# Four neighbouring tokens per partition, and a delta in three pieces, in a fused cross-covariance attention and channel-mix kernel

## The chip, the cores and the metric

One core of a Trainium2 chip runs the kernel. The metric is the device time of one execution in microseconds; three executions of the kernel before took 506.9, 507.0 and 507.39 us, and their median, 507.0 us, is the time before. The core's engines are named as the profile names them: PE (TensorE; PEld its weight loads), DVE (VectorE), ACT (ScalarE), POOL (GpSimd) and SP (SyncE). POOL and SP issue the DMAs.

## The reference

```
qn = q / (norm(q, axis=1) + 1e-6)             # q, k, v: 4 x 6208 x 256, norms over the tokens
kn = k / (norm(k, axis=1) + 1e-6)
a  = softmax(kn^T @ qn / tau)                 # 256 x 256 for each of the 4 batches
x  = v @ a                                    # 4 x 6208 x 256
x_prev = x moved by one token (zero in front of each batch)
xk = mu_k * x + (1 - mu_k) * x_prev
xr = mu_r * x + (1 - mu_r) * x_prev
out = sigmoid(xr @ w_r) * (relu(xk @ w_k)^2 @ w_v)     # w_k 256 x 1024, w_v 1024 x 256, w_r 256 x 256
```

Inputs and result are float32; the kernel computes the matmuls in bf16.

## The kernel before

**Tiling.** Each batch has 12 blocks of 512 tokens and 64 tokens left over. The blocks of all batches are taken in one list: 48 blocks, and one "left" block of 4 x 64 tokens, put ahead of the last. Channels lie on the partitions (two halves of 128), tokens along the columns.

**What happens to a block.** `v_load` (line 400, the DMA on line 403) brings 512 tokens of v into a buffer `v_bf` as bf16, on POOL's DMA queue. Today partition p holds the tokens p, 128+p, 256+p and 384+p of the block (`"(s p) c -> p s c"`), so a partition reads four rows of 1 KB that lie apart. v is then turned, so that channels are on the partitions: the first five blocks by PE (line 421, copied out of PSUM on lines 427 to 433, the blocks 2 to 4 on line 429 by DVE), all others by a transposing DMA on SP's queue (line 409). `x_stage` multiplies by the softmax matrix A (line 536, ACT copies the product to `xR`, line 542; block 0 has lines of its own, 513 to 526). `xR` is a ring of three blocks side by side, with one column in front, which holds the last token of the block before the ring's first (line 502 copies it there, or line 499 sets it to zero at the start of a batch).

`mix_stage` (line 546) makes xk and xr. Today the columns of `xR` are in the order of the tokens, so "the token before" is the column before. It takes delta = x - x_prev in one DVE instruction over both channel halves (line 576), then for k and for r multiplies delta by mu, one instruction per half (line 590), and adds x_prev (line 599). For block 0 both steps are one instruction (line 584), in two cuts of 256 columns; for the left block lines 574 and 597 do it. `mu` holds four columns, made on PE and copied out of PSUM (line 828).

`up_stage` computes xk @ w_k in four pairs of 128 hidden channels (line 628), ACT takes the relu (line 632), DVE the square (line 634). `down_stage` works on four tiles of 128 tokens: the gate's matmuls (line 682), the eight matmuls with w_v (line 689), tanh on ACT (line 693), and the product on DVE (line 695) into `res`, with tokens on the partitions. A block's `res` is stored by one DMA on SP's queue (line 709), in the same order of tokens as v was read; the last block's goes out in three parts (lines 711 and 716).

**Beside the blocks** the q and k rows of the next batch are loaded (`qk_load`, line 750, POOL's queue; each partition already reads 4 KB in one piece) and their products and norms are taken (`cov_group`: ACT squares on line 765, DVE sums on 768 to 778, PE on line 788), so that the next A is ready when its batch begins. For the first batch this is the head of the kernel (lines 323 to 387), with matmuls that only keep PE at work (line 837).

**What sets the order.** Nothing above runs in the order of the source. Every step is added to a `Plan` with an engine, a cost, a key (its due time, in units of T = 9.6 us a block), and what it reads and writes. `Plan.order` then plays the engines forward, always taking the step with the lowest key among those that are ready, and the instructions are issued in that order. A DMA in the plan takes time for its bytes on its queue; for a DMA that begins after 35.5 us of planned time the plan adds 8 us before it counts as landed, if it waits for a mark of PE's progress (a "gate") or if it is on SP's queue. POOL's loads of v and of q and k have such a gate where the mark is already known when they are added; the earliest have none. `dve(n, mode)` and `act(n)` are the plan's costs.

Of the kernel before, what the change touches and what calls it, by code (L numbers as in the profile page):

```python
# [21 lines left out]
class Plan:  # L22
# [40 lines left out]
    def order(self):  # L63
# [16 lines left out]
        while True:  # L80
# [49 lines left out]
            if s.size:  # L130
                at, took = max(bus[e], end + self.MOVE), s.size / self.RATE
                if t < 5.0:
                    at = max(at, bus["SP"])
                if e == "SP" and bus["POOL"] > at:
                    bus["POOL"] += took
                    took *= 4 if s.name == "turn v" else 2
                bus[e] = at + took
                end = bus[e] + self.LAND
                lanes[e].append(end)
                if t > self.SPARE_FROM and (s.gate or e == "SP"):  # L140
                    end += self.SPARE
# [33 lines left out]
def kernel(  # L175
# [222 lines left out]


    def v_load(n, key, gate=()):  # L400
        b, t = blocks[n]
        i = n % NV
        add("POOL", 0.75, key, lambda: nc.gpsimd.dma_start(  # L403
            v_bf[i], v[b, t * M:(t + 1) * M, :].rearrange("(s p) c -> p s c", p=P)),
            writes=[("v_bf", i)], size=M * C * 4, name="ld v", after=root0, gate=gate)
# [140 lines left out]
    def mix_stage(n, key):  # L546
# [3 lines left out]
        ki, ri = n % 2, n % 3  # L550
        o = {"k": xk[ki], "r": xr[ri]}
        cuts = [(0, 256), (256, 512)] if n == 0 else [(0, m)]
        for c0, c1 in cuts:
# [4 lines left out]
            if left:  # L558
                prev = [xl[:, dh, :, :L] for dh in range(2)]
                xdep = [("xl", b) for b in range(B)]  # L560
            else:
                prev = None
                xdep = [("x", i, 0), ("x", i, 1)]
                xdep += [("x", i - 1, 0), ("x", i - 1, 1)] if i else [("x0",)]
                if n == 1 or c0:
                    xdep += [("x1", 0, 0), ("x1", 0, 1)]
                at = i * M
# [9 lines left out]
            kd = key + c0 * .001  # L577
            unit(kd, lambda dgo=dgo, kd=kd, twice=twice, xdep=xdep: add("DVE", twice, kd, dgo, reads=xdep, writes=[("dl", di)], name="delta"))
            for which in "kr":
                km = kd + (.02 * T if which == "k" else .3 * T)  # L580
                if n == 0:
                    for dh in range(2):
                        col = dh if which == "k" else 2 + dh
                        unit(km, lambda xdep=xdep, which=which, col=col, dh=dh, c0=c0, c1=c1, km=km, w=w: add("DVE", dve(w), km, lambda: nc.vector.scalar_tensor_tensor(
                            o[which][:, dh, c0:c1], dl[di][:, dh, c0:c1], mu[:, col:col + 1], xR[:, dh, at + c0:at + c1], op0=OP.mult, op1=OP.add),
                            reads=xdep + [("dl", di), ("mu",)], writes=[("xk", ki, c0, dh) if which == "k" else ("xr", ri, dh)], name="mix"))
                    continue
                for dh in range(2):
                    col = dh if which == "k" else 2 + dh
                    unit(km, lambda col=col, dh=dh, c0=c0, c1=c1, km=km, w=w: add("DVE", dve(w, 2.77), km, lambda: nc.vector.tensor_scalar_mul(  # L590
                        dm[di][:, dh, c0:c1], dl[di][:, dh, c0:c1], mu[:, col:col + 1]), reads=[("dl", di), ("mu",)],
                        writes=[("dm", di, dh)], name="mix"))

                def mgo(which=which, c0=c0, c1=c1):
                    if left:
                        for dh in range(2):
                            nc.vector.tensor_tensor(v3(o[which][:, dh, :m]), v3(dm[di][:, dh, :m]), prev[dh], op=OP.add)
                    else:
                        nc.vector.tensor_tensor(o[which][:, :, c0:c1], dm[di][:, :, c0:c1], xR[:, :, at + c0:at + c1], op=OP.add)  # L599
                res_ = ("xk", ki, c0) if which == "k" else ("xr", ri)  # L600
                unit(km + .01, lambda mgo=mgo, km=km, twice=twice, res_=res_, xdep=xdep: add("DVE", twice, km, mgo,
                     reads=xdep + [("dm", di, 0), ("dm", di, 1)], writes=[res_] + ([("xk", 0, x, y) for x in (0, 256) for y in range(2)] if n == 2 and which == "k" else [("xr", 0, y) for y in range(2)] if n == 3 and which == "r" else []), name="mix"))

# [63 lines left out]
    def down_tile(n, s, kd, last):  # L667
# [3 lines left out]
        def go():  # L671
# [25 lines left out]
            if last:  # L697
# [7 lines left out]
                else:  # L705
                    b, t = blocks[n]
                    o = out[b, t * M:(t + 1) * M, :].rearrange("(s p) c -> p s c", p=P)
                    if n < NBLK - 1:
# [3 lines left out]
            elif n == NBLK - 1 and s:  # L712
                b, t = blocks[n]
                o = out[b, t * M:(t + 1) * M, :].rearrange("(s p) c -> p s c", p=P)
                s0 = 0 if s == 1 else 2
# [111 lines left out]
    add("PE", (0.1, 0.3), KC - 1, go, reads=[("mu_rows", 0), ("mu_rows", 1), ("ident_f",)], writes=[("vr", 1)], name="mu")  # L827
    add("DVE", TINY, KC - 1, lambda: nc.vector.tensor_copy(mu, vr[1][:, 0:4]), reads=[("vr", 1)], writes=[("mu",)], name="mu")
    softmax(0, KC)
# [116 lines left out]
```

## Time and profile before

The profiled execution took 507.02 us from end to end, and 505.1 us from the first to the last instruction (its span).

| what | profile before |
|---|---|
| time of the profiled execution, and its span | 507.02 us, 505.1 us |
| median of three runs | 507.0 us |
| granted PE clock | 1.00 |
| matmuls line 689 (down), 628 (up), 682 (gate), 536 (x), 788 (cov) | 1536, 742, 384, 188, 294 recorded |
| delta, line 576, 128x1024 bf16 | 47 times, 686 ns |
| mix, line 590 (128x512) and line 599 (128x1024) | 188 times 347 ns; 94 times 688 ns |
| DMA packets | 113,958, 77.36 MB |
| load of v (line 403), issue to landing | 48 times, median 6.3 us |
| store of a block (line 709), issue to landing | 47 times, median 5.3 us |
| load of v, time of the issue on POOL | 754 ns; a load of q or k rows 533 ns |

The busy time of an engine is the union of its instructions' times. Instructions follow each other on DVE faster than they last: an instruction's record runs on for some 0.08 us after the next one has begun, so the distance from start to start is also given where it matters. A few matmul records are missing, which shows where an engine's weight loads are all there and a matmul between them is not.

### The profile page before, as it was taken

What the parts mean: (1) busy time and instruction counts of PE and PEld (TensorE: products, weight loads), DVE (VectorE), ACT (ScalarE), POOL (GpSimd) and SP (SyncE); (2) the same over time, 40 slices, a digit from 0 to 9 for tenths busy, and PEclk for the clock granted to TensorE, in tenths of its full rate; (3) what the DMA queues carried; (4) which work ended last, traced back from release to release, by engine and by line L of the source; (5) the groups of instructions that cost most, each with busy time, mean ns of one, the idle gap of its engine ahead of it and who ended that gap; (6) DMA issues with size and microseconds to landing.
All of it is one profiled execution on the core that took longest, in us unless ns stands there. A gap on an engine that the chain in (4) does not pass through costs nothing.

```text
span 505.1 us, 9492 instructions
## 1 busy us (share of the span) xinstructions
PE 486.7 (96%) x3477; PEld 336.2 (67%) x3536; DVE 424.1 (84%) x979; ACT 407.4 (81%) x582; POOL 102.7 (20%) x174
## 2 busy tenths in 40 slices
PE   2999999999999999999999999999999999999997
PEld 0376676777676766776676676676666666666675
DVE  4569799899889989998879999899779787878974
ACT  6867799898889888888789888888767777777774
POOL 6562322222231211222121122211110111000000
PEclk9999999999999999999999999999999999999999
DMA  9999999999999999999897999996664776542123
GB/s 208 208 206 202 168 165 197 185 192 168 173 183 170 197 146 202 185 151 180 145 169 129 167 191 165 173 172 105 140 112 84 133 126 122 108 96 72 48 80 104
DMA packets 113958, 77.36 MB, mean 153 GB/s; under 512 B 49588, under 2 KB 101496, under 8 KB 113912
## 3 DMA queue, kind: packets, MB, share of 16 engines
q0 software_dynamic: 41776, 38.84, 57.0%
q1 hardware_dynamic: 72136, 37.92, 37.0%
q8 instruction: 27, 0.44, 0.4%
q14 instruction: 19, 0.16, 0.1%
HBM read 78.71 MB, written 25.43 MB: 206 GB/s over the span
## 4 chain that ended last, share of the span: by engine, by line
PE 84%; DMA 6%; DVE 6%; issue 2%; ACT 1%; POOL 0%; DVEq 0%; ACTq 0%; POOLq 0%
PE vr L689 31%; PE kT L628 30%; PE xp L536 8%; PE vr L682 8%; PE s_ps L788 6%; DMA qk<-in_q_dram 3%; DMA qk<-in_k_dram 2%; DMA v_bf<-in_v_dram 2%; DVE kk L634 1%; DVE dm L590 1%; DVE dl L576 1%; ACT kr L632 1%; DVE res L695 1%; DVE xk L599 1%; PE kT L837 0%
## 5 line engine op out<-in xcount | busy, mean ns | idle before, releaser
L632 ACT ACTIVATE kr<-kT 128x1024 bf16<-128x1024 f32 (+1 forms) x200 | 199.7, 1001 | 49.9 <-PE kT L628 46.9
L628 PE MATMUL kT<-xk,w_k 128*128 128x512 bf16 (+1 forms) x742 | 201.2, 372 | 2.7
L689 PE MATMUL vr<-w_v,kk 128*128 128x256 bf16 x1536 | 202.0, 273 | 0.1
L634 DVE TENSOR_TENSOR kk<-kr 128x1024 bf16<-128x1024 bf16 (+1 forms) x200 | 133.9, 671 | 45.2 <-ACT kr L632 45.0
L689 PEld LDWEIGHTS <-kk 128*128 128x128 bf16 x1552 | 151.6, 98 | 20.1 <-DVE kk L634 0.6
L628 PEld LDWEIGHTS <-w_k 128*128 128x128 bf16 x800 | 77.6, 98 | 51.9 <-issue 1.4
L693 ACT ACTIVATE res<-vr 128x256 f32<-128x256 f32 x192 | 74.2, 387 | 14.2 <-PE vr L689 10.3
L695 DVE SCALAR_TENSOR_TENSOR res<-res,vr 128x256 f32<-128x256 f32 x192 | 79.1, 413 | 2.5 <-ACT res L693 2.3
L682 PE MATMUL vr<-w_r,xr 128*128 128x256 bf16 x384 | 73.3, 273 | 0.1
L765 ACT ACTIVATE sq<-qk 128x2048 bf16<-128x2048 bf16 (+1 forms) x39 | 70.6, 1810 | 1.2 <-PE xp L798 0.6
L542 ACT CAST xR<-xp 128x512 bf16<-128x512 f32 x94 | 55.3, 589 | 15.2 <-PE xp L536 14.4
L403 POOL DMA_DIRECT2D v_bf<-in_v_dram x48 | 36.2, 754 | 146.8 <-PE kT L628 139.9
L682 PEld LDWEIGHTS <-xr 128*128 128x128 bf16 x384 | 37.4, 98 | 33.4
L590 DVE TENSOR_SCALAR dm<-dl,mu 128x512 bf16<-128x512 bf16 (+1 forms) x192 | 59.0, 346 | 0.4
L536 PE MATMUL xp<-vT,A 128*128 128x512 bf16 x188 | 55.9, 379 | 0.6
L788 PE MATMUL s_ps<-qk 128*128 128x256 bf16 (+1 forms) x294 | 55.5, 273 | 0.1
L750 POOL DMA_DIRECT2D qk<-in_q_dram x39 | 20.8, 533 | 100.4 <-ACT res L693 32.4
L788 PEld LDWEIGHTS <-qk 128*128 128x128 bf16 (+1 forms) x294 | 28.4, 98 | 16.2 <-issue 0.6
L576 DVE TENSOR_TENSOR dl<-xR 128x1024 bf16<-128x1024 bf16 (+1 forms) x49 | 33.1, 675 | 0.8 <-ACT xR L542 0.6
L599 DVE TENSOR_TENSOR xk<-dm,xR 128x1024 bf16<-128x1024 bf16 x47 | 32.4, 690 | 0.9
L750 POOL DMA_DIRECT2D qk<-in_k_dram x39 | 20.8, 532 | 59.6 <-PE kT L628 37.2
L599 DVE TENSOR_TENSOR xr<-dm,xR 128x1024 bf16<-128x1024 bf16 x47 | 32.2, 686 | 0.4
(94 smaller groups left out, 259.6 us busy)
## 6 DMA issues: line engine op xcount, KB each, us to landing
out_dram<-res SPq DMA_DIRECT2D x47, 512.0 KB, 5.3
v_bf<-in_v_dram POOLq DMA_DIRECT2D x48, 256.0 KB, 6.3
qk<-in_k_dram POOLq DMA_DIRECT2D x47, 256.0 KB, 7.2
qk<-in_q_dram POOLq DMA_DIRECT2D x46, 256.0 KB, 6.1
f32s<-in_q_dram SPq DMA_DIRECT2D x2, 512.0 KB, 4.3
vT<-v_bf SPq DMA_TRANSPOSE x43, 7.9
w_k<-in_moe_w_k_dram POOLq DMA_DIRECT2D x1, 512.0 KB, 9.5
w_v<-in_moe_w_v_dram POOLq DMA_DIRECT2D x1, 512.0 KB, 9.6
```

Of the source, the lines that this page charges most:

```text
L536: nc.tensor.matmul(xp, A[b][:, ih, dh * P:(dh + 1) * P], vT[o].rearrange("p (s h) q -> p h s q", h=2)[:, ih], start=ih == 0, stop=ih == 1)
L590: unit(km, lambda col=col, dh=dh, c0=c0, c1=c1, km=km, w=w: add("DVE", dve(w, 2.77), km, lambda: nc.vector.tensor_scalar_mul(dm[di][:, dh, ...
L599: nc.vector.tensor_tensor(o[which][:, :, c0:c1], dm[di][:, :, c0:c1], xR[:, :, at + c0:at + c1], op=OP.add)
L628: last = nc.tensor.matmul(kT[bk][:, x, :w], w_k[:, dh, fh * P:(fh + 1) * P], xk[n % 2][:, dh, c0:c1], start=dh == 0, stop=dh == 1)
L632: add("ACT", act(2 * w), ku + .1, lambda: nc.scalar.activation(kr[kri][:, :, :w], kT[bk][:, :, :w], AF.Relu, scale=0.5 ** 0.5), reads=[("k ...
L634: add("DVE", dve(2 * w, 2), ku + .2, lambda: nc.vector.tensor_tensor(kk[n % 2][:, 2 * p:2 * p + 2, c0:c1], kr[kri][:, :, :w], kr[kri][:, : ...
L682: nc.tensor.matmul(V[:, D:], xr[ri][:, dh, s * P:(s + 1) * P], w_r[:, dh, :], start=dh == 0, stop=dh == 1)
L689: nc.tensor.matmul(V[:, :D], kk[n % 2][:, fh, s * P:(s + 1) * P], w_v[:, fh, :], start=fh == 0, stop=fh == 7)
L693: add("ACT", act(D), kd + .3, lambda: nc.scalar.activation(r[:, s], V[:, D:], AF.Tanh, scale=0.5), reads=[bank], writes=[("res", oi, s)], ...
L695: add("DVE", dve(D), kd + .4, lambda: nc.vector.scalar_tensor_tensor(r[:, s], r[:, s], 1.0, V[:, :D], op0=OP.add, op1=OP.mult), reads=[ban ...
L765: add("ACT", act(w), key, lambda: nc.scalar.activation(Q[:rows, :, :n], G[:rows, :, :n], AF.Square), reads=both, writes=sqs, name="sq")
L788: nc.tensor.matmul(s_ps[:, ih, :], G[:rows, 1, s, ih * P:(ih + 1) * P], G[:rows, 0, s, :], start=g == 0 and s == 0 and ih == 0, stop=g == ...
```

## The change

Tokens are laid out anew for all blocks but the first and the left one. `v_load` and the stores use one new function, `tokens`: partition p holds the four neighbouring tokens 4p to 4p+3, so it reads or writes 4 KB in one piece (the last block is stored in parts, as before). Column s*128 + q of a block of x is then the token 4q + s. The token before is 128 columns back; for the first quarter (s = 0) it is in the last quarter, one column to the left of the same place; and for column 0 it is the last column of the block before. So delta becomes three instructions: columns 128 to 511, columns 1 to 127, and column 0. The first two read this block alone.

The mix now adds to x itself in place of x_prev, and `mu` holds mu - 1: x_prev + mu * delta = x + (mu - 1) * delta. Block 0 and the left block keep their order of tokens and their delta, and take the new mix as well.

In the plan the loads named "ld qk" get the 8 us whether they have a gate or not.

```diff
-                if t > self.SPARE_FROM and (s.gate or e == "SP"):
+                if t > self.SPARE_FROM and (s.gate or e == "SP" or s.name == "ld qk"):
                     end += self.SPARE
...
+    def tokens(a, n):
+
+        b, t = blocks[n]
+        return a[b, t * M:(t + 1) * M, :].rearrange("(p s) c -> p s c" if n else "(s p) c -> p s c", p=P)
+
...
-            v_bf[i], v[b, t * M:(t + 1) * M, :].rearrange("(s p) c -> p s c", p=P)),
+        add("POOL", 0.75, key, lambda: nc.gpsimd.dma_start(v_bf[i], tokens(v, n)),
...
+        dls = [("dl", di, x) for x in (0, 1, P)]
...
-                prev = [xl[:, dh, :, :L] for dh in range(2)]
-                xdep = [("xl", b) for b in range(B)]
+                own = [xl[:, dh, :, 1:] for dh in range(2)]
+                xdep = xown = [("xl", b) for b in range(B)]
             else:
-                prev = None
+                xown = [("x", i, 0), ("x", i, 1)] + ([("x1", 0, 0), ("x1", 0, 1)] if c0 else [])
...
+            if left or n == 0:
+                unit(kd, lambda dgo=dgo, kd=kd, twice=twice, xdep=xdep: add("DVE", twice, kd, dgo, reads=xdep, writes=dls, name="delta"))
+            else:
+                def step(a, b, back):
+                    nc.vector.tensor_tensor(dl[di][:, :, a:b], xR[:, :, at + 1 + a:at + 1 + b], xR[:, :, at + 1 + a - back:at + 1 + b - back], op=OP.subtract)
+                for a, b, back, cost, deps in ((P, M, P, dve(2 * (M - P), 2), xown), (1, P, 1 - 3 * P, dve(2 * P, 2), xown), (0, 1, 1, TINY, xdep)):
+                    unit(kd, lambda a=a, b=b, back=back, cost=cost, deps=deps, kd=kd: add("DVE", cost, kd, lambda: step(a, b, back),
+                                                                                       reads=deps, writes=[("dl", di, a)], name="delta"))
...
-                        nc.vector.tensor_tensor(o[which][:, :, c0:c1], dm[di][:, :, c0:c1], xR[:, :, at + c0:at + c1], op=OP.add)
+                        nc.vector.tensor_tensor(o[which][:, :, c0:c1], dm[di][:, :, c0:c1], xR[:, :, at + 1 + c0:at + 1 + c1], op=OP.add)
...
-                    o = out[b, t * M:(t + 1) * M, :].rearrange("(s p) c -> p s c", p=P)
+                    o = tokens(out, n)
...
-    add("DVE", TINY, KC - 1, lambda: nc.vector.tensor_copy(mu, vr[1][:, 0:4]), reads=[("vr", 1)], writes=[("mu",)], name="mu")
+    add("DVE", TINY, KC - 1, lambda: nc.vector.tensor_scalar_add(mu, vr[1][:, 0:4], -1.0), reads=[("vr", 1)], writes=[("mu",)], name="mu")
```

## The prediction

> **What bounds the kernel now.** I read the page first: its summary, its slices and the chain that ended last.
>
> ```profile
> span 505.1 us, 9492 instructions
> ...
> PE 486.7 (96%) x3477; PEld 336.2 (67%) x3536; DVE 424.1 (84%) x979; ACT 407.4 (81%) x582; POOL 102.7 (20%) x174
> ...
> DMA  9999999999999999999897999996664776542123
> ...
> PE 84%; DMA 6%; DVE 6%; issue 2%; ACT 1%; POOL 0%; DVEq 0%; ACTq 0%; POOLq 0%
> ```
>
> TensorE looks full, and so do the DMA engines for two thirds of the span. A busy PE need not be a PE at its pace, so I went on to the start times of its matmuls. In the chain of waits the eight 256-column matmuls of a down tile take 0.87 us, 0.109 us each; a 512-column one takes 0.216. Laying every start against the start before it plus that pace leaves, from 41.1 us to the end, five gaps on PE: at 41.46 (0.24 us), 43.28 (0.19), 49.17 (0.30), 58.15 (0.29) and 59.35 (0.13), 1.15 us together. After 60 us there are only gaps of 0.216 us, one in some 8 us; these are lost records (line 628 shows 742 matmuls and 800 weight loads), and a few of 0.1 to 0.28 us at the batch changes. So from 41 us on **PE works at its own pace, whatever the DMA share says**, and everything before 41 us is the wait for q, k and v of the first batch. The waits of PE name DMA twice, both before 41 us:
>
> ```profile
> PE vr L376 <- DVE t L364: 10.1, 4, 7.3
> PE xp L421 <- DMA v_bf<-in_v_dram: 0.3, 1, 0.3
> PE s_ps L387 <- DMA qk<-in_k_dram: 0.2, 1, 0.2
> ```
>
> The first is the head too. What could still move is in the chain of waits between 40 and 60 us, where the pipeline fills (start, us, what):
>
> ```profile
> 47.05 0.60 DVE xk L599
> 47.66 0.34 DVE kk L634
> 47.99 0.53 DVE dm L590 x2
> 48.52 0.61 DVE vT L429
> 49.13 0.04 issue
> 49.17 0.38 PE kT L628 x2
> ```
>
> VectorE runs without a pause from 40.07 past 49.17, and the last piece of that run, the copy of block 2's turned v, releases the matmuls at 49.17. **For those 9 us DVE, not PE, sets the time.** Later DVE is full in three stretches, but PE keeps its pace there (busy us; PE, PEld, DVE, ACT, POOL):
>
> ```profile
> 62.50:87.50 25.00, 24.84 (x185) 17.87 (x187) 24.84 (x56) 23.07 (x31) 5.96 (x10) 1.00 1.34 186
> 162.50:175.00 12.50, 12.45 (x90) 8.65 (x89) 12.50 (x29) 10.83 (x16) 2.87 (x5) 1.00 1.34 207
> 262.50:287.50 25.00, 24.72 (x174) 17.05 (x176) 24.96 (x60) 22.40 (x34) 4.18 (x7) 1.00 0.97 143
> ```
>
> **The change, part by part.**
>
> *Loads of v and stores of the result, four tokens to a partition.* A 512 KB block is 512 rows of 1 KB today and 128 runs of 4 KB afterwards, so 47 loads and 46 whole stores (block 0 stays as it is, the last block's store goes out in parts) lose 384 pieces each, about 36,000 of the page's 113,958 packets. Landing (median 6.3 us for v, 5.3 for the store) and POOL's issue (0.754 us for v against 0.533 for the qk loads, which already read 4 KB runs) should fall. On the path this is worth nothing: after 41 us no matmul waits for a DMA, block 0's load, which the head waits for, keeps its order, and the k loads are issued ahead of the first changed load (31.21 us). The one place left is block 1's load: its weight loads waited 0.34 us at 39.89. What follows from it, x of block 1, is used by the delta at 45.17, inside the unbroken DVE run, so the cover is that run. I take 0; bounds -0.34 and 0.
>
> *Columns of x by quarters, mix from x itself, mu less one.* The matmuls keep sizes and count; the add reads the same number of columns one place further on; the one copy into mu becomes one subtraction. The mix no longer reads the block before, which frees an x buffer earlier, but no wait is on that. 0.
>
> *Delta in three pieces* on 47 blocks (the first and the left-over block keep one). Durations: 128x1024 bf16 0.686 us, 512 elements 0.42, 256 elements 0.28, the two-element copy of line 502 0.165. From start to start in an unbroken run the same are 0.60 (45.17 to 45.77), 0.34, 0.20 and 0.12. The pieces have 768, 254 and 2 elements. By start to start: 0.47 (halfway between 0.34 and 0.60) + 0.20 + 0.12 = 0.79 against 0.60, **0.19 more a block**; by full durations 0.55 + 0.28 + 0.165 = 1.00 against 0.686, 0.31 more. Over 47 blocks 9 to 15 us more DVE work (424 becomes 433 to 439 us), off the path wherever PE has other matmuls to run. It is on the path in the run up to 49.17, which holds one such delta: +0.19 us (bounds 0, if the copy is put ahead of it, and 0.31).
>
> The second piece starts at odd columns and writes at one. [...]
>
> Later blocks: for each block I took from the timelines the start of the first down tile's seventh matmul less the end of the block's last square. Least are 0.06 us (block 1), 0.18 (block 23), 0.20 (block 12), 0.22 (block 2); most have 0.5 to 1.5. A delta 0.19 to 0.31 late eats those four slacks and no more: +0.1 us (0 to 0.6).
>
> *First rows planned later.* The planner now takes 8 us more for the first q and k rows of batch 1 (POOL 36.62 and 37.20, the only such loads without a gate after 35.5 us). These really land about 47.1 us, when the ScalarE square at 47.09 had waited 0.54 us. Their four cov steps, two matmuls each (0.22 us), now stand at 47.35, 48.66, 51.98 and 55.46. The first two lie where PE would otherwise wait for the DVE run; moved back some 8 us they leave 0.44 us idle and are done when PE has no time to spare. They may instead fill the gaps at 58.15 and 59.35 (-0.42), and the square (1.9 us ACT) and sums (0.94 us of DVE at 49.63 and 51.24) leave the crowded stretch with them; at worst all four leave holes, +0.87. Unknown between -0.42 and +0.87, I take the middle, **+0.22**. POOL's issues and SP's stores keep their places.
>
> Sum: 0 + 0.19 + 0.1 + 0.22 = +0.5 us. The profiled execution took 507.02 us, 1.92 more than its span, and stands at the median of the three runs, 507.0. So span 505.6 and **507.5 us**, 0.1% more. A measurement of this kernel tells about 0.2% (1.0 us) from no change, so this is "the same".
>
> **Rivals.**
>
> *DVE becomes the bound (slower).* In the three full stretches (62.5 us, 62.3 busy) some 6.4 blocks of 9.8 us pass. If DVE is behind there by the whole of the extra work, PE waits 6.4 x 0.19 to 0.31 = 1.2 to 2.0 us, with the other terms 508.7 to 509.5. For it: the four short slacks, three of them in or beside these stretches. Against it: in the 12.5 us before and after each stretch DVE is at 71 to 92%, the sums and carries there can wait, and the planner knows the pieces' cost. It decides once the backlog passes the 0.5 to 1.5 us of slack. I give it 0.22.
>
> *The early rows leave holes (slower by about the bound).* All four steps' time is lost, 0.87, plus 0.31 from the delta: 508.2. For it: nothing else is ready while DVE holds block 1; against: the last two of the four lie where PE is full. 0.14.
>
> *The filling gets shorter (faster).* The square and the sums leave the stretch 47 to 52 us, DVE comes to the squares of block 1 0.94 us earlier, the gaps at 49.17, 58.15 and 59.35 close: -0.72 +0.19, 506.5; all five gaps gone, 505.9. More is not there, for PE has no other idle time. 0.14.
>
> *The DMA engines were holding the kernel after all,* so that a third fewer packets bring several us. The slices say 9 of 10, but no wait names it, and the matmuls keep the same 0.87 us pace at a DMA share of 1.3 as at 0.2. Gain from the first 41 us only if the first changed loads overtake: 505.5 or less. 0.02.
>
> **How the numbers follow.** Forecast 0.48, rivals 0.22, 0.14, 0.14, 0.02. Slower by over 1.0 us: the DVE rival, half of the holes, and 0.02 of the forecast's tail, 0.31. Faster by over 1.0 us: a quarter of the third and the last, 0.05. The same: 0.64. Range 506.1 to 509.2: from most of the faster case to most of the DVE case; the forecast's own is 506.8 to 508.1.
>
> **What would show it.** Packets down to about 78,000; v's landing and POOL's issue shorter; line 576's one group replaced by three of about 0.55, 0.28 and 0.16 us, 47 each; DVE busy 433 to 439 us; the cov steps of batch 1 first at about 55 us; PE's starts still at pace after 60 us. I am wrong if matmuls after 60 us wait on squares or mixes (DVE rival), if the first up matmul is not at 41.1 us, or if the gaps before 60 us add to more than 2.2 us.

## The result, and the profile after

The kernel after the change took 528.29 us (median of six executions, 522.36 to 543.78), the kernel before beside it 508.63 us (six, 506.9 to 530.07). The ratio is 1.036 [1.028, 1.044]: slower by 3.6%, against a forecast of 507.5 us and a range that ended at 509.2. A second set of six, on another chip, gave 525.97 us (517.87 to 546.21) and 1.028 [1.022, 1.035]. Single executions of most versions, the kernel before included, can come out 10 to 30 us high; the ratios leave such disturbed runs out, and the spread stands beside each median because how often it happens is part of the story.

The profiled execution took 522.36 us, its span 520.5. From the page of the kernel after, its summary, its slices and the chain that ended last:

```profile
span 520.5 us, 9642 instructions
...
PE 494.2 (95%) x3536; PEld 336.1 (65%) x3536; DVE 432.4 (83%) x1073; ACT 407.4 (78%) x582; POOL 92.7 (18%) x174
...
PEclk9999999999998799999999999999999999999999
DMA  9999999999999999998999899999455674623123
...
DMA packets 78120, 77.37 MB, mean 149 GB/s; under 512 B 49589, under 2 KB 53625, under 8 KB 78073
...
PE 74%; DMA 17%; DVE 3%; issue 3%; ACT 2%; POOL 0%; ACTq 0%; POOLq 0%; DVEq 0%
```

Of the chain, DMA went from 6 to 17%, the granted clock fell for two slices (some 156 to 182 us), and a third fewer packets brought nothing. So I read the waits of the kernel after next (us in total, times, longest):

```profile
ACT sq L774 <- DMA qk<-in_k_dram: 7.6, 5, 2.4
...
PE kT L639 <- ACT kr L643: 6.5, 2, 4.2
...
ACT res L704 <- DMA out_dram<-res: 5.3, 2, 4.5
```

Line 774 is the square of the q and k rows, 704 the gate's tanh, 643 the relu. In the kernel before, the square waited 0.5 us for k rows, and neither of the other two waits was there:

```profile
ACT sq L765 <- DMA qk<-in_k_dram: 0.5, 1, 0.5
```

A second profile of the kernel after (`e7_after` below) has the same three waits, with 19.4 us on the k rows. Where the time went shows in PE's timeline of the kernel after (start, us, what, and in brackets the idle time before it and what ended it):

```profile
159.65 0.59 PE L639 MATMUL kT<-xk,w_k 128*128 128x512 bf16 x2 [2.28 <-ACT kr L643]
...
160.54 1.06 PE L639 MATMUL kT<-xk,w_k 128*128 128x512 bf16 x2
...
166.24 0.61 PE L539 MATMUL xp<-vT,A 128*128 128x512 bf16 x2 [1.50 <-DMA vT<-v_bf]
...
175.65 1.86 PE L639 MATMUL kT<-xk,w_k 128*128 128x512 bf16 x4 [4.24 <-ACT kr L643]
...
177.74 1.91 PE L700 MATMUL vr<-w_v,kk 128*128 128x256 bf16 x8
```

PE stands still for 2.28, 1.50 and 4.24 us, and after the first and the last of these its matmuls run at half pace: eight 256-column ones take 1.91 us where they took 1.04 at 153.94. What held the relu at 159.65 and 175.65 is in ACT's timeline, ahead of them in its queue:

```profile
155.80 1.91 ACT L774 ACTIVATE sq<-qk 128x2048 bf16<-128x2048 bf16 x1 [2.37 <-DMA qk<-in_k_dram]
...
173.81 0.38 ACT L704 ACTIVATE res<-vr 128x256 f32<-128x256 f32 x1 [4.53 <-DMA out_dram<-res]
```

In this timeline ScalarE takes its instructions one after the other. A square whose rows had not landed, and a tanh whose `res` buffer was still being stored, each held the relus behind them, and PE waits for the relus. The chain of waits gives the length of those transfers, issue to landing (the same wait, seen as start and duration):

```profile
141.03 14.69 DMA qk<-in_k_dram
...
159.85 13.87 DMA out_dram<-res
```

In the kernel before the medians were 5.8 us for the q and k rows of this line and 5.3 for a store. Why the last store began only at 159.85, 24 us after the store before it, where a block takes some 10, is in the timeline of SP, which issues the stores and the turning transfers:

```profile
124.84 10.37 SPq L412 DMA_TRANSPOSE vT<-v_bf  x1
135.31 1.54 SPq L719 DMA_DIRECT2D out_dram<-res  x1
136.95 22.81 SPq L412 DMA_TRANSPOSE vT<-v_bf  x2
159.85 0.69 SPq L719 DMA_DIRECT2D out_dram<-res  x1
```

Two turning DMAs held SP for 22.81 us while they were issued (the median issue is 1.84 us each), and the store stood behind them. The turned v itself landed 3.6 us (least), 7.9 (median) and 29.2 us (most) after its issue; before it was 3.9, 7.9 and 13.1. **So the transfers fell behind**, for a limited time. In 12.5 us windows of the kernel after (length, then busy us and instructions of PE, PEld, DVE, ACT, POOL, then granted clock, DMA share, GB/s):

```profile
150.00:162.50 12.50, 10.18 (x69) 6.54 (x68) 9.06 (x25) 9.23 (x16) 1.59 (x3) 0.92 1.21 155
162.50:175.00 12.50, 7.41 (x46) 4.56 (x45) 5.71 (x14) 4.78 (x8) 1.05 (x2) 0.91 1.25 122
175.00:187.50 12.50, 11.85 (x66) 7.29 (x66) 10.03 (x23) 9.34 (x13) 1.58 (x3) 0.76 1.12 186
187.50:200.00 12.50, 12.50 (x92) 8.72 (x90) 11.89 (x31) 9.99 (x15) 2.82 (x5) 1.00 1.24 198
```

The three windows from 150 to 187.5 lack 2.32, 5.09 and 0.65 us of PE, and by the same view 1.21 and 0.47 are missing in those from 100 and 125 us: 9.7 us idle of the 15.4 by which the span grew. Most of the rest is half pace: some 8.5 us of matmuls at half pace cost some 4 us, an estimate from their starts in the timeline. From 187.5 us on PE is full again to the end.

DMA engines that the profile calls about as busy moved less. From the packets recorded between 85 and 150 us (mean time of one packet; v and q, k rows on POOL's queue; turning and stores on SP's), with two of the experiments below:

| 85 to 150 us | GB/s | DMA share | 2048 B, rows and v | 256 B, turning v | store packet |
|---|---|---|---|---|---|
| before | 180 | 1.30 | 212 ns | 42 ns | 1024 B, 49 ns |
| after | 162 | 1.19 | 232 ns | 54 ns | 4096 B, 295 ns |
| old plan, both new orders (`e3_both`) | 184 | 1.10 | 214 ns | 35 ns | 4096 B, 169 ns |
| after with the old stores (`f1_oldstores`) | 149 | 1.21 | 245 ns | 68 ns | 1024 B, 75 ns |

At its own pace the kernel moves 180 to 184 GB/s there. The same bytes in the same packets moved at 184 GB/s in one kernel and at 162 in another. My reading is that each packet takes longer once the two queues' transfers lie over each other, and that they so stay over each other; no run shows this step by itself. I call the state of late landings and low GB/s the **backlog**. In the profiled execution it lasts from some 64 to 185 us.

### The profile page after: what moved, and what is told of

It reads as the page before. It is cut to its first block, busy times and chain, and to the rows that moved or that the text cites. A ratio compares the mean times of both kernels' runs of the same rounds, so it can differ in the third digit from the quotient of the medians.

```text
span 520.5 us, 9642 instructions
## 1 busy us (share of the span) xinstructions
PE 494.2 (95%) x3536; PEld 336.1 (65%) x3536; DVE 432.4 (83%) x1073; ACT 407.4 (78%) x582; POOL 92.7 (18%) x174
## 2 busy tenths in 40 slices
DMA packets 78120, 77.37 MB, mean 149 GB/s; under 512 B 49589, under 2 KB 53625, under 8 KB 78073
## 4 chain that ended last, share of the span: by engine, by line
PE 74%; DMA 17%; DVE 3%; issue 3%; ACT 2%; POOL 0%; ACTq 0%; POOLq 0%; DVEq 0%
PE kT L639 28%; PE vr L700 27%; DMA qk<-in_k_dram 10%; PE vr L693 7%; PE xp L539 7%; PE s_ps L797 4%; DMA qk<-in_q_dram 3%; DMA out_dram<-res 3%; DMA v_bf<-in_v_dram 2%; ACT sq L774 1%; DVE kk L645 1%; ACT kr L643 1%; PE kT L846 0%; DVE t L777 0%; PE xp L807 0%
## 5 line engine op out<-in xcount | busy, mean ns | idle before, releaser
L639 PE MATMUL kT<-xk,w_k 128*128 128x512 bf16 (+1 forms) x800 | 207.8, 375 | 8.1 <-ACT kr L643 6.5
L704 ACT ACTIVATE res<-vr 128x256 f32<-128x256 f32 x192 | 74.2, 386 | 18.6 <-PE vr L700 9.3
L545 ACT CAST xR<-xp 128x512 bf16<-128x512 f32 x94 | 55.4, 589 | 16.4 <-PE xp L539 15.9
L407 POOL DMA_DIRECT2D v_bf<-in_v_dram x48 | 26.0, 541 | 164.2 <-PE kT L639 163.1
L586 DVE TENSOR_TENSOR dl<-xR 128x768 bf16<-128x768 bf16 x141 | 42.1, 335 | 1.7 <-ACT xR L545 1.6
L777 DVE TENSOR_TENSOR t<-sq 128x1024 bf16<-128x1024 bf16 x36 | 24.8, 689 | 11.3 <-ACT sq L774 11.3
```

The costliest lines, as they stand in the source:

```text
L545: add("ACT", act(M), kx, lambda: nc.scalar.copy(xR[:, dh, at:at + M], xp), after=[m_], give="xp", writes=[("x", i, dh)], name="x evac")
L639: last = nc.tensor.matmul(kT[bk][:, x, :w], w_k[:, dh, fh * P:(fh + 1) * P], xk[n % 2][:, dh, c0:c1], start=dh == 0, stop=dh == 1)
L704: add("ACT", act(D), kd + .3, lambda: nc.scalar.activation(r[:, s], V[:, D:], AF.Tanh, scale=0.5), reads=[bank], writes=[("res", oi, s)], ...
```

## The experiments

Two theories were to be told apart. One is **the order of tokens**: the new loads or stores make transfers slower for each other. The other is **the plan**: the new order of work (the 8 us on the q and k rows, the three deltas) moves transfers so that they collide. Beside both stood VectorE's extra work. The expectations were written before each run and name the theories in their own words. In the tables a kernel counts as free of the backlog below where it takes less than 511 us.

### The orders of tokens alone, in the plan of before

The order of the instructions on all engines is that of the kernel before.

```diff
# e1_loads, against the kernel before
-  v[b, t * M:(t + 1) * M, :].rearrange("(s p) c -> p s c", p=P)
+  v[b, t * M:(t + 1) * M, :].rearrange("(p s) c -> p s c" if n else "(s p) c -> p s c", p=P)
# e2_stores, against the kernel before, both places of the block stores
-  o = out[b, t * M:(t + 1) * M, :].rearrange("(s p) c -> p s c", p=P)
+  o = out[b, t * M:(t + 1) * M, :].rearrange("(p s) c -> p s c" if n else "(s p) c -> p s c", p=P)
# e3_both: both edits
```

> The kernel before, with the order of every engine unchanged, but the loads of v (blocks 1 on) read four neighbouring tokens per partition; delta, mix and stores stay, so the tokens inside a block are mixed with the wrong neighbour and stored in another order, and the amount of work is that of before. Packet theory (v's packets of 2048 bytes, 214 ns in the trace of after, hold up the turning DMA's 256-byte packets, which share the engines, four times as long a piece as the 512-byte ones of 74 ns did): the turning DMAs land late, up to 20 us and more in place of 13.1, and the time is 515 to 530 us. Store theory and plan theory: no loss, 506 to 508 us, since stores and plan are those of before.

> The kernel before, order of every engine unchanged, but the stores (blocks 1 on) write four tokens of a partition to neighbouring rows; loads, delta and mix stay, so the rows of a block are stored in another order than computed. Store theory (packets of 4096 bytes took 270 to 287 ns between 50 and 185 us of after, four of 1024 bytes 4 x 49 before, and they stand in the same queue as the turning DMAs): 512 to 525 us. Packet theory: within 0.5% of before, since the loads keep their 512-byte packets. Plan theory: 507 us.

> The kernel before, order of every engine unchanged, with loads and stores both of four neighbouring tokens per partition; delta and mix stay, so each token is mixed with the wrong neighbour. Packet theory: like the run with the loads alone, 515 to 530 us. Store theory: like the run with the stores alone. If both count: the sum of both losses, near the changed kernel's 3.6%. Plan theory: 507 us.

The kernel before took 507.1 to 527.2 us here (seven executions, median 514.77, three below 511). The loads alone: 512.5 to 523.28 (four, median 515.05), ratio 1.014 [1.007, 1.020], none below 511. The stores alone: 506.92 to 509.39, median 507.12, ratio 1.001 [0.997, 1.004]. Both: 506.87 to 510.25, median 507.07, ratio 1.001 [0.996, 1.006]. With the new loads alone the square waits 6.3 us for k rows, in four places; the longest, from the ACT timeline of that kernel (start, us, what, idle before):

```profile
162.20 1.91 ACT L765 ACTIVATE sq<-qk 128x2048 bf16<-128x2048 bf16 x1 [4.05 <-DMA qk<-in_k_dram]
```

It is the same wait, at the same place, 160 us into the kernel, with not one instruction moved: a kernel with the new loads alone can be in the backlog. That the loads bring it is not shown by these four executions, for the kernel before had four of its seven above 511 us beside them, and none of those was profiled. With the new stores all eight executions stayed below 511, also beside the new loads (515 became 507). The 36,000 packets that both together save are worth nothing where there is no backlog, as the prediction had it.

### The new plan with the old order of tokens

```diff
# e4_plan, against the kernel after
-  return a[...].rearrange("(p s) c -> p s c" if n else "(s p) c -> p s c", p=P)
+  return a[...].rearrange("(s p) c -> p s c", p=P)
```

> The changed kernel, order of every engine unchanged, with loads and stores back in the old order of tokens; delta in three pieces and the new plan stay, so the delta is taken between wrong tokens. Plan theory (the new order of DMAs and cov steps alone makes q and k rows late): 518 to 530 us. Packet and store theories: 506.5 to 508.5 us, what the delta's extra 0.19 us a block and the moved cov steps were forecast to cost, and no matmul waiting after 60 us.

It took 507.1, 507.13, 510.78 and 520.55 us, ratio 1.002 [0.995, 1.009]; the profiled one has a span of 505.2 us, and its turned v lands at 3.9, 7.4 and 11.9 us (least, median, most). Three deltas, the new mix and the new plan together cost 0.1 us of span. So neither theory holds by itself: the old plan with both orders is at 507, the new plan with the old order is there in two of four executions and below 511 in three, and only the two together never are. VectorE's work is the same in this kernel as in the kernel after, so the rival that blamed it is out.

### Repeats, the plan without the 8 us, and smaller load packets

```diff
# e5_nospare, against the kernel after
-  if t > self.SPARE_FROM and (s.gate or e == "SP" or s.name == "ld qk"):
+  if t > self.SPARE_FROM and (s.gate or e == "SP"):
# e6_rows, against the kernel after (shortened): a block of v by two DMAs, tokens 4p, 4p+2 and 4p+1, 4p+3
-  nc.gpsimd.dma_start(v_bf[i], tokens(v, n))
+  [nc.gpsimd.dma_start(v_bf[i][:, x::2], tokens(v, n)[:, x::2]) for x in range(2)]
# e7_after: the kernel after again; e3_again: e3_both again
```

> The changed kernel without the 8 us that the plan adds for the first q and k rows; everything else is kept. Interaction theory: the plan's shift of the cov steps counts for part of the loss, 508 to 518 us, if it is this part of the plan that collides, and 518 to 530 if it is the delta's. Disturbance theory: the same as the changed kernel within 0.5 us, 506.5 to 508.5 at rest; the first cov step then stands at about 47 us and may wait up to 0.5 us for its rows.

> The changed kernel, but each load of v comes as two DMAs of alternate rows, so that its pieces are 1 KB reads and 512-byte packets again; order and layout are kept. Packet theory in its milder form (2048-byte packets of v hold up the turning DMAs only when transfers are slow): under disturbance less time than the changed kernel of the same rounds by 5 us or more, and turning DMAs landing within 14 us; at rest the same, 506.5 to 508.5. Disturbance theory: no difference from the changed kernel in either. Two more issues on POOL, 0.5 us each, are hidden.

> The changed kernel once more, on another occasion. Interaction theory (old order of tokens with the new plan took 507.1 us at best, new layout with the old plan 506.9, so the loss needs both: the new plan places its transfers where runs of 4 KB collide): 518 to 530 us in every run, beside a kernel before of 507. Disturbance theory (the transfers were slow from outside during the measurement; the kernel before took 510 to 530 us in 7 of its last 10 runs too): within 0.3% of the kernel before wherever that one stands at 507, thus 506.5 to 508.5, and both far above in the same rounds.

> The new layout of loads and stores under the old plan, delta and mix once more (tokens are mixed with the wrong neighbour). Interaction theory: 506.5 to 508 us, 10 to 20 us less than the changed kernel of the same rounds. Disturbance theory: within 1 us of the changed kernel at rest, and no better than it under disturbance.

| kernel | median (range), us | below 511 us | ratio |
|---|---|---|---|
| before | 507.31 (506.7 to 527.56) | 25 of 29 | |
| `e7_after` | 525.97 (517.87 to 546.21) | 0 of 6 | 1.028 [1.022, 1.035] |
| `e5_nospare` | 506.70 (506.45 to 538.97) | 8 of 12 | 0.999 [0.996, 1.001] |
| `e6_rows` | 507.86 (507.63 to 510.3) | 12 of 12 | 1.002 [1.001, 1.003] |
| `e3_again` | 506.79 (506.53 to 516.04) | 8 of 12 | 1.002 [0.998, 1.005] |

Two quite different edits each take the loss away. Without the 8 us the kernel is at 506.6 in most executions and above 511 us in four of twelve. With v in packets of 512 bytes (96,920 packets in all) and the plan with the 8 us kept, none of twelve is; this edit also reads memory in runs of 1 KB again and puts 47 more issues on POOL (134.9 us busy in place of 92.7), and no run parts these from the packets. From the page of `e5_nospare`, the chain that ended last, by line:

```profile
PE vr L700 33%; PE kT L639 32%; PE vr L693 8%; PE xp L539 8%; PE s_ps L797 6%; DMA qk<-in_q_dram 3%; DMA qk<-in_k_dram 2%; DMA v_bf<-in_v_dram 2%; PE xp L807 1%; ACT kr L643 1%; PE kT L846 0%; PE kT L700 0%; DVE kk L645 0%; POOL qk L350 0%; PE xp L314 0%
```

The packets are the same in number and size, and DMA has 6 to 7% of the chain, as before, in place of 17.

The profiled execution of `e3_again` took 516.04 us. It is the program of `e3_both`, with the same bytes, packets and order of instructions, and it moved 162 GB/s between 85 and 150 us where `e3_both` moved 184, with 49 ns for a turning packet in place of 35. Its waits are those of the kernel after:

```profile
ACT sq L765 <- DMA qk<-in_k_dram: 10.2, 6, 5.6
...
PE kT L628 <- ACT kr L632: 7.0, 2, 4.3
```

So the old plan does not rule the backlog out, it makes it rarer (12 of 16 executions of this program are below 511 us, none of 12 of the kernel after). And it need not begin at 60 us: here the first two turnings landed after 8.5 and 7.1 us, as in a good execution, and the late ones are those of 110 and 130 us, after 13.6 and 20.8.

### Which part of the burst at 60 us

In the profiled execution of the kernel after the backlog begins where the turning DMAs begin. SP issues block 0's store at 60.15 us and two turnings at 60.63 and 63.05; POOL issues q rows at 61.05 and k rows at 64.10. In two-microsecond windows of the kernel after:

```profile
64.00:66.00 2.00, 2.00 (x21) 1.45 (x19) 2.00 (x8) 1.93 (x3) 0.53 (x1) 1.00 1.17 49
66.00:68.00 2.00, 1.69 (x15) 1.29 (x14) 2.00 (x5) 2.00 (x3) 0.53 (x1) 1.00 1.17 69
68.00:70.00 2.00, 2.00 (x15) 1.29 (x14) 2.00 (x6) 1.14 (x3) 0.53 (x1) 1.00 1.41 105
```

and the same of `e4_plan`, whose instructions stand alike, within 0.1 us:

```profile
64.00:66.00 2.00, 2.00 (x21) 1.46 (x19) 2.00 (x7) 1.93 (x3) 0.53 (x1) 1.00 1.36 178
66.00:68.00 2.00, 1.69 (x16) 1.26 (x14) 2.00 (x5) 2.00 (x3) 0.76 (x1) 1.00 0.97 175
68.00:70.00 2.00, 2.00 (x15) 1.32 (x14) 2.00 (x6) 1.15 (x3) 0.53 (x1) 1.00 1.17 153
```

The last two columns matter: at a like DMA share, 49, 69 and 105 GB/s against 178, 175 and 153. In the kernel after single 256-byte packets of a turning took 1.3 to 2.5 us around 64 us, and the first two turnings landed after 11.0 and 15.9 us, in `e4_plan` after 7.4 and 7.2. So the next kernels moved this meeting.

```diff
# f1_oldstores, against the kernel after: the stores in the old order
-  o = tokens(out, n)
+  o = out[...].rearrange("(s p) c -> p s c", p=P)
# f2_pooldelay, g3_delay4: POOL fills two, or four, unused tiles before the q load of 61.05
+  if b == 1 and g == 4 and not x:
+      for f in f32s:                       # g3_delay4: f32s + f32s
+          nc.gpsimd.memset(f, 0.0)
# f3_best: e5_nospare and e6_rows together (the code here is shortened)
# f4_late, against e5_nospare: SP's work of 1.6 us from block 0's store on is issued 1.6 us later
+  moved = [s for s in seq if s.eng == "SP" and first.start <= s.start < first.start + 1.6]
+  moved[0].gate = list(moved[0].gate) + ups[-1:]
# g1_swap (against the kernel after), g4_swap5 (against e5_nospare): block 0's store behind two turnings
+  seq.remove(sp[k])
+  seq.insert(seq.index(sp[k + 2]) + 1, sp[k])
# g2_copy, against the kernel after: a plain copy in place of each turning DMA
-  nc.sync.dma_start_transpose(vT[o], v_bf[i].rearrange("p s c -> p (s c)"))
+  nc.sync.dma_start(vT[o].rearrange("p a b -> p (a b)"), v_bf[i].rearrange("p s c -> p (s c)"))
```

> The changed kernel, order of every engine kept, with the stores alone back in the old order (rows of a block are stored in another order than computed). Backlog theory (from about 60 us the turning DMAs' 256-byte packets stand behind others and never catch up; a turn has some 65 packets on an engine, and 65 x (220 + 40) ns = 17 us beside a stream of 2048-byte packets): if the stores' 4096-byte packets start the backlog (the first turn landed in 11.0 us behind such a store, in 7.4 us behind one of 1024-byte packets), 507 to 510 us; if v's 2048-byte packets alone keep it up, 515 to 530 us. I take the second for likelier, since with v in 512-byte packets and new stores the first turn took 10.7 us too and yet the time was 507.9.

> The changed kernel with two fills of the unused f32 buffers put ahead of one load of q rows (that of 61.05 us) on POOL's queue, some 1.5 to 2 us, and nothing else changed. Backlog theory with a first collision (block 0's store at 60.15 and the first turn at 60.63 meet the q load of 61.05; without the plan's 8 us the store stood at 58.84, 2.1 us ahead of the load): the first turns land within 9 us again, 506.5 to 509 us in most runs. Plan theory (the other order of PE, ACT and DVE up to 100 us does it): unchanged, 518 to 530 us.

> The changed kernel without the plan's 8 us and with v in two DMAs of alternate rows (1 KB reads, 512-byte packets). Backlog theory: 506.2 to 507.2 us and no run above 511, where the changed kernel without the 8 us alone had runs of 518 to 539. If v's packets have no part in it: 506.7 with the same outliers.

> The changed kernel without the plan's 8 us (506.7 us), order of every engine kept, but block 0's store, with the turns behind it on SP's queue, made to wait for a pair of matmuls about 1.6 us later. Backlog theory with a first collision: turns of 11 us and more from the first on, 515 to 530 us in most runs. Plan theory: 506.5 to 507 us, as without the wait, since no other engine waits for that store for 20 us.

| kernel | median (range), us | below 511 us | ratio |
|---|---|---|---|
| before, beside these | 510.26 (508.46 to 522.65) | 6 of 9 | |
| `f1_oldstores` | 529.76 (525.0 to 542.84) | 0 of 5 | 1.037 [1.032, 1.043] |
| `f2_pooldelay` | 522.2 (507.35 to 528.29) | 1 of 5 | not given |
| `f3_best` | 507.58 (507.56 to 507.8) | 5 of 5 | 0.996 [0.994, 0.998] |
| `f4_late` | 507.46 (506.8 to 530.93) | 3 of 5 | 0.995 [0.991, 0.998] |

With the old stores the loss is all there, so the stores' 4 KB packets are not what brings it. The waits of that kernel are again those of the backlog, the stores' buffers first:

```profile
ACT res L704 <- DMA out_dram<-res: 15.0, 3, 7.2
...
ACT sq L774 <- DMA qk<-in_k_dram: 4.5, 4, 2.5
```

`f2_pooldelay` told nothing about a delay: its two fills ran in time in which POOL was idle (59.35 to 61.2 us), and the load went out at 61.14 in place of 61.05. `f4_late` failed its expectation. Store at 60.98, q rows at 61.25, first turning at 61.45: nearly the meeting of the kernel after, and yet three of five executions stayed clear, with 184, 157 and 192 GB/s between 64 and 70 us in the profiled one. In it the q load was ahead of the turning, in the kernel after behind it. That a store, a turning and a q load meet at 61 us is thus not enough. And one execution of five of `f2_pooldelay` stayed clear with the load moved by 0.09 us only, so that none of twelve for the kernel after need not mean never.

> The changed kernel with block 0's store put behind the first two turning DMAs on SP's queue; every other queue and engine keeps its order. Burst theory (three turns back to back behind that store, 60.6 to 68 us, meet two loads, and from 64 to 70 us the DMA engines move 49 to 105 GB/s while they count as busy; the backlog lives on from there): turns start near 57 us, one at a time, 506.5 to 510 us. Steady theory (new v loads and turns get into each other's way wherever they meet, the start does not matter): 518 to 530 us as before.

> The changed kernel with each turning DMA of v replaced by a plain DMA copy of the same bytes on the same queue; the blocks from 5 on then multiply v that is not turned. If it is the turning DMA that loads hold up (and that holds up loads: single 256-byte packets of it took 1.3 to 2.5 us at 64 us): no backlog, 506 to 507.5 us in all runs. If the sum of bytes and requests is too much for the DMA engines: 515 to 530 us.

> The changed kernel with four fills of unused buffers, about 3.7 us of POOL, ahead of the q load of 61.05 us (two fills ended at 61.2 and moved it by 0.1 us only). The load then comes at about 63 us, when the first turn has run for 2.5 us. First-collision theory: 506.5 to 510 us. Steady theory: 518 to 530 us; the collision is only put off.

> The changed kernel without the plan's 8 us and with block 0's store behind the first two turns. Burst theory: 506.4 to 507 us and no run above 512 (without the swap 4 of 12 runs lay between 518 and 539). Steady theory: 506.5 us with the same outliers.

| kernel | median (range), us | below 511 us | ratio |
|---|---|---|---|
| before, beside these | 508.08 (506.68 to 532.41) | 20 of 33 | |
| `g1_swap` | 509.18 (506.81 to 527.37) | 6 of 11 | 1.002 [0.997, 1.007] |
| `g2_copy` | 506.97 (506.74 to 507.12) | 11 of 11 | 0.997 [0.995, 1.000] |
| `g3_delay4` | 507.33 (506.87 to 520.84) | 8 of 11 | 0.998 [0.995, 1.002] |
| `g4_swap5` | 507.37 (506.39 to 533.18) | 6 of 11 | 1.000 [0.995, 1.004] |

On this chip even the kernel before was clear in only 20 of 33. Against 0 of 12 for the kernel after (on two other chips), the two kernels that keep its plan and its packets and move only what meets at 61 us are much better: 8 of 11 with the q load at 63.24 in place of 61.05, 6 of 11 with the first two turnings at 51.74 and 56.09, ahead of the store. The first meeting matters, then, in many executions. It is not the only place: the profiled execution of `g1_swap` (512.75 us) has its first turning that lands after more than 13 us at 159.3 us (18.5). In `g4_swap5`, where the plan was good already, the swap bought nothing; its profiled execution, of 527.89 us, has the waits of the backlog (18.6 us on k rows) in the plan without the 8 us.

The clearest is `g2_copy`: the same plan, the same loads and stores, as many bytes moved on SP's queue, but by plain copies in place of turnings. The copies also go in packets of 2048 bytes where the turnings have 256, so that the whole kernel has 38,903 packets in place of 78,120. Eleven of eleven lie within 0.4 us of each other. From the groups of its tile of turned v:

```profile
L412 SPq DMA_DIRECT2D vT<-v_bf x43: 464/471/1867, 60.5 to 453.0; - x43
DMA to landing us min/median/max: 2.8/6.1/8.8
```

and from the same view of the kernel after:

```profile
L412 SPq DMA_TRANSPOSE vT<-v_bf x43: 1237/1842/11778, 60.6 to 468.3; - x43
DMA to landing us min/median/max: 3.6/7.9/29.2
```

The first line has the time of the issue (least, median, most, in ns), the second the landing. A copy is out of SP's way in 0.47 us and lands within 8.8; a turning holds SP up to 11.8 us. **Without the turning DMAs there is no backlog.** Whether it is the turning itself, its small packets or the time that it takes of the DMA engines, this run does not tell: DMA share in the stretch from 87.5 to 162.5 us is 0.85 to 0.91 here, against 1.15 to 1.22 in the kernel after.

### What the runs show together

Medians in us, and how many executions were below 511:

| | old plan | plan with the 8 us |
|---|---|---|
| old loads, old stores | 507.31, 25 of 29 (before; 514.77, 3 of 7 beside `e1_loads` to `e4_plan`) | 508.96, 3 of 4 (`e4_plan`) |
| new loads, old stores | 515.05, 0 of 4 (`e1_loads`) | 529.76, 0 of 5 (`f1_oldstores`) |
| old loads, new stores | 507.12, 4 of 4 (`e2_stores`) | not tried |
| new loads, new stores | 507.07 and 506.79, 12 of 16 (`e3_both`, `e3_again`) | 528.29 and 525.97, 0 of 12 (after) |

Shown: the loss of the kernel after needs the new loads of v (in 512-byte packets it is gone in 12 of 12 executions, with the old order of tokens in 3 of 4), it needs the turning DMAs with their 256-byte packets (copies: gone in 11 of 11), and, with the new stores beside the new loads, it needs the times at which the plan lets transfers meet (without the 8 us, or with the q rows 2 us later: gone in most executions). VectorE has no part in it. Not shown: that the new loads cost anything in the old plan, where `e1_loads` is at 1.014 [1.007, 1.020] beside a kernel before that was itself above 511 in four of seven. Open: what happens inside the DMA engines. Why a 256-byte packet takes 1.3 to 2.5 us around 64 us is not settled, and such a stretch is no proof by itself: the kernel before moved 84 and 78 GB/s between 64 and 68 us in its profiled execution of 507.02 us, and `e6_rows` 64, 76 and 82 between 64 and 70, with its first turnings landing after 10.7 and 12.9 us. Both recovered. Nor do long packets tell: between 85 and 150 us a turning packet took 53 ns in `e6_rows`, as in the kernel after (54), and yet it moved 179 GB/s. The size of v's packets seems to decide whether a backlog that has begun goes away; that is argued from this one kernel, not shown.

No version beats the kernel before beyond doubt. `e5_nospare` has the lowest median, 506.7, which is not told from the kernel before (0.999 [0.996, 1.001]), and was above 511 us in 4 of 12 executions against 4 of 29. All five executions of `f3_best` lie within 0.3 us, and it was 0.4% better than the kernel before on its chip, 0.996 [0.994, 0.998], but there the kernel before stood at 510.26; against the 506.7 of `e5_nospare` it is some 1 us behind.

## Why the prediction was wrong

**What bounds the kernel now: half right.** PE did work at its own pace, and the first 41 us were the head. "So from 41 us on PE works at its own pace, whatever the DMA share says" is true as an observation and was used as a bound. No wait on a DMA meant no loss yet; it did not mean room. The kernel before is itself above 511 us in some executions (4 of 29 on one chip, 13 of 33 on another), by its times alone, for none of these was profiled. Neither its DMA share (1.34 from 62.5 to 87.5 us, 1.30 from 85 to 150) nor its longest landing of 13.1 us could have told how near it stood: `e6_rows`, which stays below 511 in twelve of twelve, has 1.32 from 85 to 150 us and a longest landing of 16.6.

**Loads of v and stores of the result: the step that failed.** It said: "On the path this is worth nothing: after 41 us no matmul waits for a DMA", with bounds of -0.34 and 0. There was no bound on the side of a loss. In the plan that the change has, they cost some 20 us: 528.29 against 507.1 to 510.78 for three of the four executions of `e4_plan`, which has the same plan and the old order of tokens, and 1.037 [1.032, 1.043] with the loads alone (`f1_oldstores`). The forecasts of packets (about 78,000; 78,120) and of the issue of v on POOL (0.533 us; 0.541 mean) came true. The landing times that "should fall" did so where there is no backlog: in `e3_both` v lands after 5.6 us in place of 6.3, a block's store after 4.4 in place of 5.3. In the kernel after the medians stayed, 6.2 and 5.5, while the longest grew, for a store from 12.8 to 17.7 us and for the turned v from 13.1 to 29.2. The longer time of the other queue's 256-byte packets (54 ns in the kernel after, 42 in the kernel before, between 85 and 150 us) was a cost that the term did not have: I asked what each transfer costs by itself, not what it does to the transfers beside it.

**First rows planned later: the other half.** The term had +0.22 us within -0.42 to +0.87, from PE's gaps alone. For PE it was sound: the steps moved to 55.37 us, as forecast, the gaps at 58.15 and 59.35 us are gone, and with the old order of tokens the whole new plan costs 0.1 us of span. "POOL's issues and SP's stores keep their places" holds for their order; their times against each other moved by up to a microsecond (from block 0's store to the q load at 61 us: 1.7 us before, 0.9 after), and with the new packets all twelve executions of the kernel are above 511 us. The two edits are each worth nothing, or nearly so, and together some 20 us: I had summed them as if they were apart.

**Delta in three pieces: right.** From the groups of the kernel after, by form:

```profile
L586 DVE TENSOR_TENSOR dl<-xR 128x768 bf16<-128x768 bf16 x47 | 26.1, 555 | 1.7 <-ACT xR L545 1.6
L586 DVE TENSOR_TENSOR dl<-xR 128x254 bf16<-128x254 bf16 x47 | 13.5, 288 | 0.0
L586 DVE TENSOR_TENSOR dl<-xR 128x2 bf16<-128x2 bf16 x47 | 7.7, 163 | 0.0
```

0.555, 0.288 and 0.163 us against 0.55, 0.28 and 0.165; DVE busy 432.4 us, just below the forecast's 433 to 439. The piece with an odd output column takes 0.288 us for 254 elements, where 256 took 0.279 (line 590) and 0.287 (line 574) in the kernel before: no cost of the odd column shows.

**Mix and mu: right**, at nothing; no wait is on them.

**The rivals.** DVE as the bound: its condition, matmuls after 60 us that wait for squares or mixes, was not met; PE's new waits are on relus, and those on transfers. Holes: there are none; counted as the prediction counts, PE has four gaps from 41.1 to 60 us (0.25 and three of 0.19), 0.8 us together, against 1.15 before. Shorter filling: half of what this rival wanted is there, 0.34 of its 0.72 us, but with the same gaps the span of `e4_plan` is 505.2 us, no shorter than 505.1. "The DMA engines were holding the kernel after all" was the only rival with DMA in it, at 0.02 and with the sign the other way. The case that came, transfers that fall behind because of the change, had no place among the cases.

## What to carry to other kernels

That no engine waits for a DMA does not show that the DMA engines have room: give any edit of packet sizes or of issue times a bound on the side of a loss. Afterwards read the GB/s moved and the longest landing and issue beside the medians. Fewer, larger packets helped the queue that had them (v landed after 5.6 us in place of 6.3 in `e3_both`), and in the kernel after the transfers of small packets on another queue, those of a transposing DMA, landed after up to 29.2 us in place of 13.1; test the edit both in the old order of work and in the new one. When a kernel can fall into such a state, one median says little: run it often, and compare both the lowest times and the share of executions that reach them.

## What the runs showed of the hardware that was not expected

- Transfers on two queues had two states at the same bytes and the same packet sizes, each lasting for tens of us: 184 GB/s with 35 ns a turning packet (`e3_both`), or 162 GB/s with 49 ns in another execution of the same program (`e3_again`) and 54 ns in the kernel after. The DMA share of the page is no measure of which: 1.10, 1.16 and 1.19, and 1.30 in the kernel before.
- By an estimate, most of the time of a turning was not that of its own packets. The kernel after has 49,589 packets under 512 bytes, `g2_copy` 4,868, 1040 fewer for each of the 43 turnings, or 65 for each of the 16 engines as a mean. At the 54 ns a packet of the kernel after and the 42 of the kernel before, both between 85 and 150 us, 65 of them one after the other take 3.5 and 2.7 us. Between 94 and 150 us the turnings of the kernel after landed after 18 to 29 us, those of the kernel before after 8 to 13. What the rest of that time is, and whether it is a wait for packets of the loads of v (232 ns each with 2048 bytes in the kernel after, 98 with 512 in the kernel before), no run shows: in `e3_both`, with the same packets as the kernel after, all 43 turnings landed within 11.7 us. Nor does one show why the packets themselves grow from 35 to 54 ns.
- A turning DMA held the queue that issues it for 1.2 us at least and, in the backlog, for up to 11.8, so that a store in the same queue was late by more than its own transfer.
- PE idle for 2.28 us, and again for 4.24, ran at half pace afterwards for some 3.5 and 5 us: the granted clock was 0.50 from 161 to 163 and from 175 to 180 us (0.92 to 0.76 as the mean of the windows above). After the 1.50 us idle before 166.24 it was 1.00 from 166 to 170, and eight 256-column matmuls took 1.04 us again.
